# Attention and a squared-ReLU layer on one core: k and q of the first batch turned together, and a remainder made by a product with a negative identity

## The chip, the cores and the metric

The program runs on one core of one Trainium2 chip. The metric is the time of one execution on the device in microseconds (us), the median of three runs. One more execution was taken with a profiler; all rows shown are from it.

## What is computed

```python
rms = sqrt(mean(x * x, axis=-1, keepdims=True) + 1e-06)       # for q and k, over 64 elements
q_n, k_n = q / rms * g_q, k / rms * g_k
scores = q_n @ k_n.T / 8
attn = softmax(scores)                                        # over the keys
x = (attn @ v), heads side by side                            # 3584 x 768
h = maximum(x @ w_in, 0)                                      # 3584 x 2048
out = (s * h * h + b) @ w_out                                 # 3584 x 768
```

There are 8 batches of 12 heads, each with 448 rows of 64 elements. All is float32, `w_in` and `w_out` come as float64 and are read as pairs of 32-bit words.

## The kernel before

**Pairs and slots.** Two heads make a pair, six pairs a batch, 48 pairs in all; `j` is the head of a pair, 0 (the even head) or 1. The order of all work is written out by hand in slots: a pair has eight (`W = 8`), slot 8p the first of pair p, four for each head, and 22 slots lead in. In slot s TensorE is given, in this order: the two `st` products of slot s (`score_t`, L451 and L454: scores with the keys on the partitions), the transposes of a turn if one is due (L278), the `sh` product of slot s + 10 (`score`, L410: scores with the queries on the partitions, for their maximum), and `av` of slot s - 2 (`weigh`, L513: the exponents times v). ScalarE is given first the exponent of slot s (L466), which waits for `st` of the same slot. Then come the next steps of the jobs already begun, then the jobs that begin in this slot, then on VectorE `maximum` of slot s + 10 (L421), and last the jobs called late, the conversions of w_in among them. Every engine runs its queue in the order given.

**Products of two parts.** TensorE takes float32 in a faster rounded form (float32r). So k and q are split in a high part, the rounded copy, and a low part, the difference: `ka` holds k_hi in its partitions 0 to 63 and k_lo in 64 to 127, `qa` q_hi in both halves, and `qb` q_lo.

**The first batch and three pairs more (pairs 0 to 8)** read q and k by rows: `load_rows`, then `norm_rows` squares on ScalarE (L261), sums on VectorE (L266), makes the inverse root and multiplies on GpSimd (L269 to L271). `turn`, fourteen slots ahead of the head's first slot, transposes them on TensorE into two banks of PSUM, `tk` of k and `tk` of q, by four transposes of 112 x 64 each. `split_turned` follows in three steps, one a slot: ScalarE copies k_hi (L286) and scales q_hi (L287); ScalarE scales q_hi again into the other half (L289) and VectorE subtracts k_lo (L290); VectorE makes q_lo (L293). Then the banks are free. PSUM has eight banks, handed out from one list in the order in which they come free; `st`, `sh`, `av`, `tk`, `ph` and the words of w_in (`bits`) share it.

**Beside it** w_in is converted in 24 pieces: four steps on VectorE (L135, L138, L140, L143) and two on ScalarE (L136, L149) over five slots; `PACE` is the list of slots in which a piece begins. From slot 56 on a slot also carries six `ffn_in` products (L208) of the batch before. Pairs from 9 on (`NR`) are read in another way (`load`, `norm`, L348, L353). `split_x` (L562, L563) splits a group of the attention's result for `ffn_in`; `invert` and `divide` come before it and divide by the softmax sums.

Of the kernel before, what the change touches and what calls it, by code (L numbers as in the profile page):

```python
# [39 lines left out]
OUT = (92, *range(110, 141, 6), *(48 * b + i for b in range(3, 8) for i in range(14, 43, 7)))  # L40


@with_exitstack
def attention_then_relu2_ffn(
# [197 lines left out]
    if True:  # L242
# [8 lines left out]

        def load_rows(p, j):
            tag = f"{('kq', 'rb')[p % 2]}{j}"
            raw = raws[p, j] = ap.tile([QC, 2, NQ, D], F32, tag=tag, name=f"rows{p}_{j}")
            nc.sync.dma_start(raw, rows0[p, :, j])

        def norm_rows(p, j):
            raw = raws[p, j].rearrange("p t c d -> p (t c) d")
            n = 2 * NQ
            sq = lp.tile([QC, n, D], F32, tag="al", bufs=2, name=f"sq{p}_{j}")  # L260
            S.activation(  # L261
                sq.rearrange("p i d -> p (i d)"), raw.rearrange("p i d -> p (i d)"), AF.Square
            )
            yield
            ssq = ap.tile([QC, n], F32, tag="ssq", bufs=2, name=f"ssq{p}_{j}")
            V.tensor_reduce(out=ssq, in_=sq, op=ALU.add, axis=AX.X)  # L266
            yield
            ri = ap.tile([QC, n], F32, tag="ri", bufs=2, name=f"ri{p}_{j}")
            G.tensor_scalar(ri, ssq, 1.0 / D, 1e-6, ALU.mult, ALU.add)  # L269
            G.tensor_tensor(ri, ri, mhalf[:QC, :n], ALU.pow)  # L270
            G.tensor_tensor(raw, raw, ri.unsqueeze(2).broadcast_to([QC, n, D]), ALU.mult)  # L271

        def turn(p, j):
            raw = raws.pop((p, j))
            for t in range(2):
                tk, bank = psum(f"tk{p}_{j}_{t}")
                for c in range(NQ):
                    T.transpose(  # L278
                        tk[:D, c * QC : (c + 1) * QC], raw[:, t, c], ident[:QC, :QC]
                    )  # L280
                tks[p, j, t] = tk[:D, :SEQ], bank

        def split_turned(p, j):
            n, a = p % 2, slice(j * SEQ, (j + 1) * SEQ)
            (k, k_bank), (q, q_bank) = (tks.pop((p, j, t)) for t in range(2))
            S.copy(ka[n][:D, a], k)  # L286
            S.activation(qa[n][:D, a], q, AF.Copy, scale=gqk[:D])  # L287
            yield
            S.activation(qa[n][D:, a], q, AF.Copy, scale=gqk[:D])  # L289
            V.tensor_tensor(ka[n][D:, a], k, ka[n][:D, a].bitcast(F32), ALU.subtract)  # L290
            free.append(k_bank)
            yield
            V.scalar_tensor_tensor(  # L293
                qb[n][:D, a], q, gqk[:D], qa[n][:D, a].bitcast(F32), ALU.mult, ALU.subtract
            )
            free.append(q_bank)

        def load_kq(p, j):
            t = kqs[p, j] = ap.tile([P, 2, SEQ], F32, tag=f"kq{j}", name=f"kq{p}_{j}")
# [324 lines left out]
                next(g)  # L624
                loaded.append(g)

        def convert(n):


            g = loaded[0] if n == 0 else turning[0]  # L630
            if n == 0:
                turning.append(loaded.pop(0))
            for _ in range((2, 1, 1, 2, 1)[n]):
                next(g, None)
            if n == 4:
                turning.pop(0)

        turning = []

        late = (convert, convert_out, invert)  # L640

        fill = iter(())

# [11 lines left out]
        for p in range(NPAIR):  # L655
            s0 = W * p
            if p >= NR:
                at(s0 - 32, load, p)
                at(s0 - 28, norm, p)
                at(s0 - 24, keep, p)  # L660
            for j in range(2):
                s1 = s0 + 4 * j
                if p >= NR:
                    at(s1 - 19, load_kq, p, j)
                    at(s1 - 19, spread, p, j)
                    at(s1 - 15, scale, p, j)
# [15 lines left out]
            at(s0 + 13, invert, p)  # L682
            at(s0 + 14, divide, p, 1)
            at(s0 + 16, divide, p, 2)
            at(s0 + 18, divide, p, 3)
        for b in range(B):
            for g in range(NP):
                at(end(b + 1) - (2 if b < B - 1 else 4) + g, split_x, b, g)
        for s_ in (FIRST, FIRST + 3):
            at(s_, load_piece)  # L690
        for s_ in PACE:
            for n in range(5):
                at(s_ + n, convert, n)
            at(s_ + 3, load_piece)

        for s_ in OUT:
            at(s_ - 5, load_out)
# [371 lines left out]
```

## Time and profile before

| what | value |
| --- | --- |
| median of three runs | 1401.3 us (1400.87 to 1402.17) |
| the profiled execution | 1402.48 us |
| its span, from first to last instruction | 1400.7 us |
| TensorE (PE) busy | 1379.6 us, 98% |
| VectorE (DVE) busy | 1038.5 us, 74% |
| ScalarE (ACT) busy | 868.8 us, 62% |
| GpSimd (POOL) busy | 1021.7 us, 73% |
| mean granted TensorE clock | 0.996 |

PE is the matmul, PEld the load of its weights (they overlap), SP the engine that issues the DMAs. A row of the timeline has the start in us from the span's start, the duration, engine, source line, operation, the tiles written and read, shapes and count, and in brackets the idle time before it and what ended it. A row of a view by line has the count, the busy time and the mean of one in ns, and then the idle time before them with its releasers. The lines (L451) are those of the kernel before; in the kernel after, the same statements stand 3 to 19 lines lower.

### The profile page before, as it was taken

How to read it: one execution, taken by the hardware profiler on the slowest of the kernel's cores; microseconds unless marked ns; L12 is line 12 of the kernel's file. 1: busy time of each engine (PE TensorE's matmuls, PEld its weight loads, DVE VectorE, ACT ScalarE, POOL GpSimd, SP SyncE). 2: the span in 40 equal slices, each digit the busy share in tenths (PEclk: the TensorE clock that was granted, in tenths of full speed). 3: DMA queues.
4: the chain of work that ended last, by engine and by line, in shares of the span. 5: the costliest groups of instructions: out<-in, count | busy, mean ns of one | idle time of the engine just before them, and what ended most of it. 6: DMA issues, size and time to landing. Idle time of an engine off the chain costs nothing. (4 is left out here: it accounts for less than half of the span.)

```text
span 1400.7 us, 22180 instructions
## 1 busy us (share of the span) xinstructions
PE 1379.6 (98%) x6976; PEld 1262.0 (90%) x6976; DVE 1038.5 (74%) x1603; ACT 868.8 (62%) x1658; POOL 1021.7 (73%) x940
## 2 busy tenths in 40 slices
PE   7999999999999999999999999999999999999998
PEld 5666888999999899999989989989999999999998
DVE  8999786888888778788788778565766665666655
ACT  5776666777777776776777777654544444444443
POOL 7687788777877787777787776267767777577763
PEclk8999999999999999999999999999999999999999
DMA  5566886777677677677677766354434333233331
GB/s 148 133 174 175 258 242 192 220 239 226 190 238 217 200 235 218 189 228 239 198 219 214 225 188 204 94 160 150 118 91 121 99 99 98 84 120 98 98 97 62
DMA packets 209253, 237.95 MB, mean 170 GB/s; under 512 B 72848, under 2 KB 187024, under 8 KB 209136
## 3 DMA queue, kind: packets, MB, share of 16 engines
q1 hardware_dynamic: 209136, 236.54, 57.6%
q8 instruction: 55, 0.90, 0.3%
q14 instruction: 62, 0.51, 0.1%
HBM read 178.00 MB, written 47.11 MB: 161 GB/s over the span
## 5 line engine op out<-in xcount | busy, mean ns | idle before, releaser
L208 PE MATMUL ph<-x,wih 128*128 128x448 f32 x1536 | 491.7, 366 | 0.5 <-DVE x L563 0.5
L848 PE MATMUL m<-t,gh 128*128 128x384 f32 x1568 | 399.3, 335 | 0.2
L208 PEld LDWEIGHTS ph<-x,wih 128*128 128x128 f32 x1536 | 288.6, 188 | 30.8 <-issue 6.7
L421 DVE TENSOR_REDUCE nmx<-sh 112x1 fp32r<-112x448 f32 x384 | 236.6, 618 | 85.3 <-PE sh L410 82.5
L208 PE MATMUL ph<-x,wil 128*128 128x448 f32 x768 | 294.0, 383 | 0.0
L848 PEld LDWEIGHTS m<-t,gh 128*128 128x128 f32 x1568 | 283.4, 188 | 1.0 <-DVE ot L863 0.9
L470 ACT ACTIVATE st<-st 128x448 f32<-128x448 f32 (+1 forms) x294 | 154.2, 524 | 192.9 <-PE st L454 189.9
L848 PE MATMUL m<-t,gl 128*128 128x384 f32 x784 | 262.6, 335 | 0.3 <-DVE gl L830 0.3
L829 ACT CAST gh<-g 128x896 fp32r<-128x896 f32 x112 | 105.4, 942 | 178.2 <-POOL g L819 178.2
L830 DVE TENSOR_TENSOR gl<-g,gh 128x896 fp32r<-128x896 f32 x112 | 127.7, 1141 | 107.2 <-ACT gh L829 107.2
L815 POOL TENSOR_TENSOR g<-g 128x256 f32<-128x256 f32 x112 | 94.6, 845 | 113.5 <-DVE g L814 113.5
L513 PE MATMUL av<-ah,vs 128*128 128x448 f32 x576 | 164.9, 367 | 0.8 <-DVE al L491 0.5
L451 PE MATMUL st<-qa,ka 128*128 128x448 f32 (+1 forms) x384 | 159.1, 414 | 4.1 <-DVE nmx L421 4.0
L208 PEld LDWEIGHTS ph<-x,wil 128*128 128x128 f32 x768 | 144.3, 188 | 17.9 <-issue 6.7
L478 ACT CAST ah<-st 128x448 fp32r<-128x448 f32 (+1 forms) x294 | 156.8, 533 | 1.3
L555 POOL TENSOR_TENSOR u<-uz,zb 64x448 f32<-64x448 f32 x96 | 126.7, 1320 | 42.1 <-DMA zb<-z_d 38.3
L410 PE MATMUL sh<-ka,qa 128*112 128x448 f32 x384 | 145.5, 382 | 3.6 <-DVE ka L290 1.8
L848 PEld LDWEIGHTS m<-t,gl 128*128 128x128 f32 x784 | 147.1, 188 | 0.6 <-DVE gl L830 0.6
L491 DVE TENSOR_TENSOR al<-st,ah 128x448 fp32r<-128x448 f32 x216 | 132.7, 614 | 18.7 <-ACT ah L478 15.8
L454 PE MATMUL st<-qb,kb 128*128 128x448 f32 (+1 forms) x384 | 140.4, 366 | 0.0
L394 POOL TENSOR_TENSOR ka<-kq,ka 64x448 fp32r<-64x448 f32 x78 | 95.5, 1224 | 57.0 <-ACT ka L391 52.3
L819 POOL TENSOR_TENSOR g<-g 128x256 f32<-128x256 f32 x112 | 125.9, 1124 | 0.0
(93 smaller groups left out, 2398.2 us busy)
## 6 DMA issues: line engine op xcount, KB each, us to landing
kq<-in_dram SPq DMA_DIRECT2D x78, 448.0 KB, 4.9
rb<-i_d SPq DMA_DIRECT2D x78, 448.0 KB, 5.9
r_d<-r SPq DMA_DIRECT2D x128, 224.0 KB, 3.1
raw<-in_dram SPq DMA_DIRECT2D x39, 448.0 KB, 5.1
raw<-r_d SPq DMA_DIRECT2D x64, 256.0 KB, 2.8
w64i<-in_dram SPq DMA_DIRECT2D x24, 512.0 KB, 4.7
w64o<-in_dram SPq DMA_DIRECT2D x32, 384.0 KB, 4.6
kb<-ka SPq DMA_DIRECT2D x96, 112.0 KB, 3.3
```

Of the source, the lines that this page charges most:

```text
L208: T.matmul(ph[:, :SEQ], w[:, cc, f0 : f0 + P], xs[b, cc][:, part, :], start=n == 0, stop=n == 3 * NCC - 1,)
L410: T.matmul(sh[:QC, :SEQ], qa[p % 2][:, a].rearrange("k (p c) -> k c p", c=NQ)[:, c], ka[p % 2][:, a], start=True, stop=True,)
L421: V.tensor_reduce(out=nmxs[p][:, c : c + 1], in_=sh[:QC, :SEQ], op=ALU.max, axis=AX.X, negate=True)
L451: T.matmul(st[:rows, :SEQ], ka[n][:, keys], qa[n][:, q], start=True, stop=False)
L454: T.matmul(st[:rows, :SEQ], kb[n][:, keys], qb[n][:, q], start=False, stop=True,)
L470: S.activation(st[:rows, :SEQ], st[:rows, :SEQ], AF.Exp)
L478: S.copy(ah[:rows], sts[i][0][:rows, :SEQ])
L491: V.tensor_tensor(al, st[:rows, :SEQ], ah[:rows].bitcast(F32), ALU.subtract)
L513: T.matmul(av[:, :SEQ], x, a, start=kc == 0 and m == 0, stop=kc == 3 and m == len(todo) - 1,)
L555: G.tensor_tensor(u[a], uzs.pop((p, j))[a], zb[a], ALU.mult)
L830: V.tensor_tensor(gl, g9[:, 1:8], gh.bitcast(F32), ALU.subtract)
L848: T.matmul(to, g[:, sa], w, start=m == 0 and n == 0, stop=m == NM - 1 and n == 2,)
```

## The change

**The joint turn.** `rows0` is laid out so that k and q of one row lie side by side, and `turn` transposes 112 x 128 at a time: four transposes and one bank, with k in its partitions 0 to 63 and q in 64 to 127. The bank is given back when all of `split_turned` has read it.

**k_lo in PSUM.** For the even head of pairs 2 to 8 (`in_bank`), `less_hi` adds the product of `ka` and a negative identity (`less`, 64 x 64 in a 128 x 128 tile of zeros) to the turned bank, so that k - k_hi stands where k stood; ScalarE then copies it to `ka` (L311 of the kernel after), in the third step of `split_turned` in place of the subtraction in the second. The product is called late in the slot of the second step, that is, behind `sh` and ahead of `av`, and writes all 128 partitions of the bank (adding zeros to q).

**The order.** `norm_rows` comes two slots earlier from pair 2 on; the first `load` of `NR` ten slots earlier; three of the later pieces of w_in begin later and all of them keep their order; the first piece of w_out eight slots later; `invert` and `divide` of the first five pairs one to three slots later; the last `split_x` of batch 0 one slot later.

```diff
-PACE = (-15, -10, *range(1, 61, 5), *range(59, 89, 3))
+PACE = (-15, -10, *range(1, 56, 5), 60, 63, 66, 69, 72, 74, 77, 79, 82, 84, 87)
...
+    less = cpool.tile([P, P], F32R, name="less")
+    G.memset(less.bitcast(F32), 0.0)
+    S.activation(less[: P // 2, : P // 2], ident[: P // 2, : P // 2], AF.Copy, scale=-1.0)
...
         def turn(p, j):
             raw = raws.pop((p, j))
-            for t in range(2):
-                tk, bank = psum(f"tk{p}_{j}_{t}")
-                for c in range(NQ):
-                    T.transpose(
-                        tk[:D, c * QC : (c + 1) * QC], raw[:, t, c], ident[:QC, :QC]
-                    )
-                tks[p, j, t] = tk[:D, :SEQ], bank
+            tk, bank = psum(f"tk{p}_{j}")
+            for c in range(NQ):
+                T.matmul(
+                    tk[:, c * QC : (c + 1) * QC],
+                    raw[:, c].rearrange("p t d -> p (t d)"),
+                    ident[:QC, :QC],
+                    start=c == 0, stop=not in_bank(p, j) and c == NQ - 1, is_transpose=True,
+                    skip_group_check=True,
+                )
+            tks[p, j] = tk, bank
+
+        def in_bank(p, j):
+            return p >= 2 and j == 0
+
+        def less_hi(p, j):
+            n, a = p % 2, slice(j * SEQ, (j + 1) * SEQ)
+            T.matmul(
+                tks[p, j][0][:, :SEQ], less, ka[n][:, a],
+                start=False, stop=True, skip_group_check=True,
+            )
...
             S.copy(ka[n][:D, a], k)
-            S.activation(qa[n][:D, a], q, AF.Copy, scale=gqk[:D])
+            S.activation(qa[n][D:, a], q, AF.Copy, scale=gqk[D:])
             yield
-            S.activation(qa[n][D:, a], q, AF.Copy, scale=gqk[:D])
-            V.tensor_tensor(ka[n][D:, a], k, ka[n][:D, a].bitcast(F32), ALU.subtract)
-            free.append(k_bank)
+            S.activation(qa[n][:D, a], q, AF.Copy, scale=gqk[D:])
+            if not in_bank(p, j):
+                V.tensor_tensor(ka[n][D:, a], k, ka[n][:D, a].bitcast(F32), ALU.subtract)
             yield
+            if in_bank(p, j):
+                S.copy(ka[n][D:, a], k)
...
-                at(s0 - 32, load, p)
+                at(s0 - (42 if p == NR else 32), load, p)
...
-                    at(s1 - 21, norm_rows, p, j)
+                    at(s1 - (21 if p < 2 else 23), norm_rows, p, j)
                     at(s1 - 14, turn, p, j)
                     at(s1 - 13, split_turned, p, j)
+                    if in_bank(p, j):
+                        at(s1 - 12, less_hi, p, j)
```

How it moves instructions, at the even head of pair 5. On TensorE, from the `st` products of slot 26 to those of slot 28 and what follows, before:

```order
L278 MATMUL tk5_0_0_958<-ident_66,rows5_0_670 64x112 x4
L278 MATMUL tk5_0_1_963<-ident_66,rows5_0_670 64x112 x4
L410 MATMUL sh36_968<-ka0_198,qa0_200 112x448
L513 MATMUL av3_0_975<-e24_913,vf3_814 128x448
L451 MATMUL st27_977<-qa1_201,ka1_199 128x448
L454 MATMUL st27_977<-qb1_205,kb1_203 128x448
L410 MATMUL sh37_992<-ka0_198,qa0_200 112x448
L513 MATMUL av3_0_975<-e25_934,vf3_814 128x448
L451 MATMUL st28_997<-qa1_201,ka1_199 128x448
L454 MATMUL st28_997<-qb1_205,kb1_203 128x448
L410 MATMUL sh38_1008<-ka0_198,qa0_200 112x448
```

and after:

```order
L280 MATMUL tk5_0_915<-ident_66,rows5_0_642 128x112 x4
L429 MATMUL sh36_920<-ka0_201,qa0_203 112x448
L532 MATMUL av3_0_927<-e24_874,vf3_779 128x448
L470 MATMUL st27_929<-qa1_204,ka1_202 128x448
L473 MATMUL st27_929<-qb1_208,kb1_206 128x448
L429 MATMUL sh37_946<-ka0_201,qa0_203 112x448
L532 MATMUL av3_0_927<-e25_891,vf3_779 128x448
L470 MATMUL st28_951<-qa1_204,ka1_202 128x448
L473 MATMUL st28_951<-qb1_208,kb1_206 128x448
L429 MATMUL sh38_959<-ka0_201,qa0_203 112x448
L294 MATMUL tk5_0_915<-ka1_202,less_74 128x448
L532 MATMUL av3_0_927<-e26_904,vf3_779 128x448
```

Eight transposes became four, and the product (L294) stands behind `sh38` and ahead of `av` of slot 26. In the built program it waits for ScalarE's second q copy of this head (L306 below).

On ScalarE, from the exponent of slot 27 (`e27`) to that of slot 29, before:

```order
L466 ACTIVATE e27_980<-st27_977 128x448
L286 CAST ka1_199<-tk5_0_0_958 64x448
L287 ACTIVATE qa1_201<-tk5_0_1_963,gqk_214 64x448
L261 ACTIVATE sq6_0_990<-rows6_0_839 112x512
L466 ACTIVATE e28_1000<-st28_997 128x448
L289 ACTIVATE qa1_201<-tk5_0_1_963,gqk_214 64x448
L466 ACTIVATE e29_1017<-st29_1014 128x448
L149 CAST wih1_716<-wai7_1011 128x512
```

and after:

```order
L485 ACTIVATE e27_932<-st27_929 128x448
L303 CAST ka1_202<-tk5_0_915 64x448
L304 ACTIVATE qa1_204<-tk5_0_915,gqk_217 64x448
L485 ACTIVATE e28_954<-st28_951 128x448
L306 ACTIVATE qa1_204<-tk5_0_915,gqk_217 64x448
L485 ACTIVATE e29_969<-st29_966 128x448
L311 CAST ka1_202<-tk5_0_915 64x448
L264 ACTIVATE sq6_1_976<-rows6_1_879 112x512
L152 CAST wih1_682<-wai7_963 128x512
```

The squares of `norm_rows` left the place ahead of `e28`, and the copy of k_lo (L311) came in behind `e29`.

On VectorE, around the same head, before:

```order
L290 TENSOR_TENSOR ka1_199<-tk5_0_0_958,ka1_199 64x448
L266 TENSOR_REDUCE ssq6_0_1004<-sq6_0_990 112x8
L421 TENSOR_REDUCE nmx4_889<-sh38_1008 112x1
L143 SCALAR_TENSOR_TENSOR wai7_1011<-wih1_716,bits7_971 128x512
L293 SCALAR_TENSOR_TENSOR qb1_205<-tk5_0_1_963,gqk_214,qa1_201 64x448
L421 TENSOR_REDUCE nmx4_889<-sh39_1026 112x1
```

and after:

```order
L440 TENSOR_REDUCE nmx4_846<-sh38_959 112x1
L146 SCALAR_TENSOR_TENSOR wai7_963<-wih1_682,bits7_923 128x512
L312 SCALAR_TENSOR_TENSOR qb1_208<-tk5_0_915,gqk_217,qa1_204 64x448
L440 TENSOR_REDUCE nmx4_846<-sh39_980 112x1
L269 TENSOR_REDUCE ssq6_1_990<-sq6_1_976 112x8
```

The subtraction (L290) is gone, and q_lo (L312), which waited for the second q copy (L289), waits in the built program for the copy of k_lo (L311). At an odd head VectorE's subtraction (L308) stays; it now waits for the second q copy (L306), where L290 waited for L286.

More of the change, by code (lines that the diff above doesn't have):

```diff
@@ L32 @@
 FILL = (2, 2, 2)
-PACE = (-15, -10, *range(1, 61, 5), *range(59, 89, 3))
+PACE = (-15, -10, *range(1, 56, 5), 60, 63, 66, 69, 72, 74, 77, 79, 82, 84, 87)
 GAP = 2
 STEPS = {0: 2, 1: 3, 2: 4, 3: 5, 5: 6, 6: 7, 8: 8, 9: 9, 11: 10, 12: 11, 13: 12}
-OUT = (92, *range(110, 141, 6), *(48 * b + i for b in range(3, 8) for i in range(14, 43, 7)))
+OUT = (100, *range(110, 141, 6), *(48 * b + i for b in range(3, 8) for i in range(14, 43, 7)))
 @with_exitstack
@@ L253, in load_rows @@
             tag = f"{('kq', 'rb')[p % 2]}{j}"
-            raw = raws[p, j] = ap.tile([QC, 2, NQ, D], F32, tag=tag, name=f"rows{p}_{j}")
+            raw = raws[p, j] = ap.tile([QC, NQ, 2, D], F32, tag=tag, name=f"rows{p}_{j}")
             nc.sync.dma_start(raw, rows0[p, :, j])
         def norm_rows(p, j):
-            raw = raws[p, j].rearrange("p t c d -> p (t c) d")
+            raw = raws[p, j].rearrange("p c t d -> p (c t) d")
             n = 2 * NQ
@@ L274, in turn @@
             raw = raws.pop((p, j))
-            for t in range(2):
-                tk, bank = psum(f"tk{p}_{j}_{t}")
-                for c in range(NQ):
-                    T.transpose(
-                        tk[:D, c * QC : (c + 1) * QC], raw[:, t, c], ident[:QC, :QC]
-                    )
-                tks[p, j, t] = tk[:D, :SEQ], bank
+            tk, bank = psum(f"tk{p}_{j}")
[16 more added lines that the diff above has]
+            )
         def split_turned(p, j):
             n, a = p % 2, slice(j * SEQ, (j + 1) * SEQ)
-            (k, k_bank), (q, q_bank) = (tks.pop((p, j, t)) for t in range(2))
+            tk, bank = tks[p, j]
+            k, q = tk[:D, :SEQ], tk[D:, :SEQ]
             S.copy(ka[n][:D, a], k)
-            S.activation(qa[n][:D, a], q, AF.Copy, scale=gqk[:D])
+            S.activation(qa[n][D:, a], q, AF.Copy, scale=gqk[D:])
             yield
-            S.activation(qa[n][D:, a], q, AF.Copy, scale=gqk[:D])
-            V.tensor_tensor(ka[n][D:, a], k, ka[n][:D, a].bitcast(F32), ALU.subtract)
-            free.append(k_bank)
+            S.activation(qa[n][:D, a], q, AF.Copy, scale=gqk[D:])
+            if not in_bank(p, j):
+                V.tensor_tensor(ka[n][D:, a], k, ka[n][:D, a].bitcast(F32), ALU.subtract)
             yield
+            if in_bank(p, j):
+                S.copy(ka[n][D:, a], k)
             V.scalar_tensor_tensor(
-                qb[n][:D, a], q, gqk[:D], qa[n][:D, a].bitcast(F32), ALU.mult, ALU.subtract
+                qb[n][:D, a], q, gqk[D:], qa[n][D:, a].bitcast(F32), ALU.mult, ALU.subtract
             )
-            free.append(q_bank)
+            free.append(bank)
         def load_kq(p, j):
@@ L625, in load_piece, with convert @@
                 loaded.append(g)
-        def convert(n):
-            g = loaded[0] if n == 0 else turning[0]
+        def convert(n, at_):
             if n == 0:
-                turning.append(loaded.pop(0))
+                turning[at_] = loaded.pop(0)
             for _ in range((2, 1, 1, 2, 1)[n]):
[L634 to L640, printed above, removed]
+                next(turning[at_], None)
+        turning = {}
+        late = (convert, convert_out, invert, less_hi)
         fill = iter(())
@@ L681, in attention_then_relu2_ffn @@
                 at(s0 + 3, split_v_rest, p)
[L682 to L685, printed above, removed]
+            wait = (0, 0, 0, 0) if p >= NP else (0, 1, 1, 1) if p == NP - 1 else (1, 2, 2, 3)
+            at(s0 + 13 + wait[0], invert, p)
+            for n in range(3):
+                at(s0 + 14 + 2 * n + wait[n + 1], divide, p, n + 1)
         for b in range(B):
             for g in range(NP):
-                at(end(b + 1) - (2 if b < B - 1 else 4) + g, split_x, b, g)
+                at(end(b + 1) - (2 if b < B - 1 else 4) + g + (b == 0 and g == NP - 1), split_x, b, g)
         for s_ in (FIRST, FIRST + 3):
@@ L692, in attention_then_relu2_ffn @@
             for n in range(5):
-                at(s_ + n, convert, n)
-            at(s_ + 3, load_piece)
+                at(s_ + n, convert, n, s_)
+            at(s_ + (3 if s_ < 60 else 2), load_piece)
         for s_ in OUT:
@@ L1052 @@
     rows0 = _np.stack([a.reshape(n, 2, 4, s // 4, d)[:9] for a in (k, q)], 2)
-    rows0 = rows0.transpose(0, 4, 1, 2, 3, 5)
+    rows0 = rows0.transpose(0, 4, 1, 3, 2, 5)
     laid = [kq, rows, rows0, vs, g] + [_np.asarray(inputs[x]) for x in _INS]
```

## The prediction

> **What bounds the kernel now.** I read the stretches of the windows view first, then who waited for whom on TensorE, then the timeline of single slots. After its first batch the kernel is a full TensorE: the busy time in stretches of 20 us, with the columns PE, PEld, DVE, ACT, POOL (each with its instructions), clock, DMA share and GB/s:
>
> ```profile
> core 0: us, PE busy (x) PEld busy (x) DVE busy (x) ACT busy (x) POOL busy (x), PEclk, DMA share, GB/s
> ...
> 20.00:40.00 20.00, 18.16 (x75) 12.98 (x74) 19.68 (x34) 15.87 (x31) 13.76 (x17) 0.87 0.48 129
> 40.00:60.00 20.00, 18.62 (x82) 12.99 (x80) 18.33 (x32) 14.47 (x30) 14.21 (x17) 1.00 0.46 120
> ...
> 100.00:120.00 20.00, 17.35 (x74) 11.36 (x72) 17.80 (x32) 14.86 (x29) 15.81 (x19) 1.00 0.67 165
> 120.00:140.00 20.00, 17.94 (x74) 13.76 (x73) 17.83 (x27) 12.35 (x24) 13.33 (x13) 1.00 0.71 188
> 140.00:160.00 20.00, 20.00 (x87) 16.21 (x87) 14.33 (x25) 12.31 (x24) 16.25 (x15) 1.00 0.89 269
> ```
>
> From 140 us on TensorE has no idle time. The change adds and removes nothing there, so the end moves by what the first batch gains or loses. In the first batch VectorE is as full as TensorE. The start of a slot is the weight load of its first `st` product (L451); the first row here is slot 3, the second slot 60, and 61 and 62 follow:
>
> ```profile
> 28.97 0.19 PEld L451 LDWEIGHTS st<-qa,ka 128*128 128x128 f32 x1 [0.19 <-PE sh L410]
> ...
> 134.07 0.19 PEld L451 LDWEIGHTS st<-qa,ka 128*128 128x128 f32 x1
> ...
> 136.66 0.19 PEld L451 LDWEIGHTS st<-qa,ka 128*128 128x128 f32 x1
> 139.22 0.19 PEld L451 LDWEIGHTS st<-qa,ka 128*128 128x128 f32 x1
> ```
>
> Slot 3 to slot 60 is 105.1 us. How long TensorE needs for it by itself comes from three rows: a slot without a turn, slot 28, and a turn of eight transposes, slot 30:
>
> ```profile
> 71.19 0.19 PEld L451 LDWEIGHTS st<-qa,ka 128*128 128x128 f32 x1 [0.19 <-issue]
> 71.56 0.19 PEld L454 LDWEIGHTS st<-qb,kb 128*128 128x128 f32 x1 [0.19 <-issue]
> 71.77 0.28 PEld L410 LDWEIGHTS sh<-ka,qa 128*112 128x112 f32 x1
> 71.97 0.39 PEld L513 LDWEIGHTS av<-e,vf 128*128 128x128 f32 x2
> 72.54 0.19 PEld L451 LDWEIGHTS st<-qa,ka 128*128 128x128 f32 x1 [0.19 <-ACT qa L287]
> 73.91 0.19 PEld L451 LDWEIGHTS st<-qa,ka 128*128 128x128 f32 x1 [0.19 <-issue]
> 74.49 0.89 PEld L278 LDWEIGHTS tk<-ident,rows 112*64 112x64 f32 x8
> ```
>
> A slot is 1.36 us ((73.91 - 71.19) / 2), a turn adds 0.89, and a slot with six `ffn` products is 2.57 ((139.22 - 134.07) / 2). The 57 slots are 53 of the first kind (3 to 55), with 13 turns (slots 6, 10 ... 54), and four of the last (56 to 59): 72.1 + 11.6 + 10.3 = 94.0 us. So TensorE lost 11.1 us to waits, and mostly VectorE ended them, as TensorE's own list of waits for these 105 us says (engine, line, releaser: us, times, longest):
>
> ```profile
> PEld st L451 <- DVE nmx L421: 7.3, 10, 2.6
> ...
> PEld sh L410 <- DVE wai L143: 1.8, 2, 1.2
> ```
>
> A PSUM bank comes free when `maximum` or a conversion of w_in has read it, and VectorE is late with that. The two largest single ones, slots 47 and 59, and what stood ahead of the first:
>
> ```profile
> 102.31 0.95 ACT L348 ACTIVATE raw<-raw 128x896 f32<-128x896 f32 x1 [1.64 <-DMA raw<-in_dram]
> ...
> 105.03 0.19 PEld L451 LDWEIGHTS st<-qa,ka 128*128 128x128 f32 x1 [2.61 <-DVE nmx L421]
> ...
> 131.58 0.19 PEld L451 LDWEIGHTS st<-qa,ka 128*128 128x128 f32 x1 [2.23 <-DVE nmx L421]
> ```
>
> **The change part by part.** The profiled execution took 1402.48 us, a span of 1400.7 and 1.8 outside it; the median of the three runs is 1401.3, so I work out a difference and put it on the median.
>
> *The joint turn.* Eight transposes with 64 columns of weights become four with 128. What a step of TensorE's queue costs here is the weight load:
>
> ```profile
> L278 PEld LDWEIGHTS tk<-ident,rows 112*64 112x64 f32 x104 | 10.3, 111 | 2.0 <-DVE nmx L421 0.6
> ...
> L451 PEld LDWEIGHTS st<-qa,ka 128*128 128x128 f32 x58 | 11.0, 189 | 15.8 <-DVE nmx L421 7.3 <-issue 4.3 <-ACT qa L287 1.7
> ...
> L278 PE MATMUL tk<-ident,rows 112*64 112x112 f32 x104 | 12.3, 259 | 0.4 <-DVE nmx L421 0.4
> ```
>
> 8 x 0.111 = 0.89 becomes 4 x 0.189 = 0.76: 0.13 a turn, **-1.7** over 13 turns. The bounds: a joint load at the price of a small one (0.111) gives 13 x 0.444 = -5.8; four transposes at the recorded 0.259 of one give 1.04 a turn, +1.9. I take 0.189, since it is a load of the same 128 columns. The Trainium skill (TensorE: Matmul & The Clock Gate, "LDWEIGHTS (loading the stationary operand)") prices a load by its columns alone, columns / 1.2 ns. By that eight loads of 64 cost what four of 128 cost, and this term would be 0 instead of -1.7; the trace disagrees, 111 ns for 64 columns being far over half of 189 for 128. The five turns ahead of slot 3 are counted at nothing: they wait for `norm_rows` on GpSimd. So are the memset and the negative identity, in the wait for the first rows.
>
> *The product with the negative identity*, seven times (pairs 2 to 8, slots 4, 12 ... 52). Its own time is a product of 448 columns, 0.20 (71.97 - 71.77). It stands in TensorE's queue between `sh` and `av` of its slot, and it may not write the bank before ScalarE has read q from it for the second time. That copy stands behind the `exponent` of the same slot, which waits for the `st` product issued 0.6 us earlier. In slot 28, TensorE's second `st` product, and then ScalarE from slot 27's exponent on:
>
> ```profile
> 71.76 0.36 PE L454 MATMUL st<-qb,kb 128*128 128x448 f32 x1
> ```
>
> ```profile
> 70.87 0.54 ACT L466 ACTIVATE e<-st 128x448 f32<-128x448 f32 x1 [0.84 <-PE st L454]
> 71.31 0.51 ACT L286 CAST ka<-tk 64x448 fp32r<-64x448 f32 x1
> 71.72 0.63 ACT L287 ACTIVATE qa<-tk,gqk 64x448 fp32r<-64x448 f32 x1
> 72.25 0.62 ACT L261 ACTIVATE sq<-rows 112x512 f32<-112x512 f32 x1
> 72.77 0.53 ACT L466 ACTIVATE e<-st 128x448 f32<-128x448 f32 x1
> 73.32 0.63 ACT L289 ACTIVATE qa<-tk,gqk 64x448 fp32r<-64x448 f32 x1
> ```
>
> `norm_rows` (L261) moves two slots earlier, so its row goes from this place and the exponent runs when both ScalarE (72.25) and `st` (72.12) are done: 72.25. The second q copy starts 0.55 later (73.32 - 72.77) and takes 0.63: 73.43. The product could have started at 71.97. So TensorE waits 1.4 us, plus 0.2 of its own, plus about 0.1 for a weight load that no product covers after a wait (an estimate: half of 0.19): 1.7 x 7 = **+11.9**. Behind it in TensorE's queue stand `av` of slot 26 and all of slot 29; ScalarE then waits for `st` of slot 29, and VectorE for `sh`. Bounds: no wait at all, 7 x 0.2 = +1.4; above, the next term.
>
> *Conversions of w_in on ScalarE* fall into the slot ahead of the product in slots 11, 19 and 51, between the first copies and the exponent. Such a step is 0.62 to 0.67:
>
> ```profile
> L136 ACT ACTIVATE wih<-w64i 128x512 fp32r<-128x512 f32 x11 | 7.4, 674 | 0.0
> ...
> L149 ACT CAST wih<-wai 128x512 fp32r<-128x512 f32 x11 | 6.8, 617 | 8.9 <-DVE wai L143 8.8
> ```
>
> The copies there leave ScalarE no slack against a slot of 1.36 (70.87 to 72.25, 1.38, from one exponent to the next without L261), so each adds about 0.6: **+1.8**, between 0 and 2.0.
>
> *The waits that go.* VectorE loses seven subtractions (0.618 each, 4.3 us), and up to slot 60 the conversion that began in slot 56 with half of that of slot 59 (six steps of 0.69, 4.1 us):
>
> ```profile
> L290 DVE TENSOR_TENSOR ka<-tk,ka 64x448 fp32r<-64x448 f32 x14 | 8.7, 618 | 1.0 <-ACT ka L286 0.6
> ...
> L135 DVE TENSOR_SCALAR bits<-w64i 128x512 int32<-128x512 int32 x12 | 8.2, 680 | 0.0
> ```
>
> The rows of pair 9 are asked for ten slots earlier, which takes away the 1.64 of DMA in front of slot 47's wait. While TensorE stands at the product, VectorE catches up. Against that stands a new wait: the q_lo step of an even head (L312) now follows k_lo's copy on ScalarE (L311), and `maximum` of its slot, a sum of squares and a conversion queue behind it on VectorE; TensorE needs the banks that these free two slots later. That copy ends about one exponent and one copy after `st` of slot 29, some 1 us, and VectorE, having caught up, stands for 1 to 2 us. An odd head's subtraction likewise follows the second q copy. Of the 11.1 us I keep 2.3 and let 8.8 go: **-8.9**, rounded. Bounds: 0.5 kept (one short wait in all), or 6 kept (over half of what VectorE and the banks cost now).
>
> *At nothing.* ScalarE's seven copies (0.51 each) come in time that it waits anyway behind the product. The conversions that now come later are wanted at slot 92 (the last starts at 87, five slots of 2.57 ahead). The divisions, one to three slots later, meet their split in slot 60 and the first product with it in slot 61; if that cover is gone TensorE waits about a us there. SP's queue carries the same transfers, pair 9's first load ten slots earlier.
>
> The sum: -1.7 + 11.9 + 1.8 - 8.9 = **+3.1 us**: 1405.6 for the profiled execution and 1404.4 on the median, 0.22% slower. A difference under 0.2% (2.8 us) can hardly be told from none here.
>
> **The rivals.** *The waits just change places*: the same chain, but nearly all 11.1 us go, since VectorE always has time to catch up. With 0.5 kept the sum is +1.3 and the time 1402.6. For it: VectorE's work falls by 8.4 us while TensorE's stretch grows. Against: the two new waits of VectorE on ScalarE.
>
> *VectorE becomes the bound through the wait for L311.* It is idle up to 1.6 us in each of seven pairs, 11 us, where it was free for 6.4 of the 80 us of the four first-batch rows above; if it comes to L312 more than a slot late, `maximum` falls behind and the bank waits stay, 6 kept: +6.8, 1408.1. It decides from the point where VectorE's rest after a product is shorter than its wait at L312.
>
> *The product does not wait* (the faster side): its operands are there when TensorE comes to it, because TensorE comes late for other reasons. Then 7 x 1.4 = 9.8 fall away: -6.7, 1394.6. For it: TensorE did lose 11.1 us. Against: none of that was in slots of this kind; slot 28 above ran its bare 1.36, and the exponent cannot run ahead of its own `st`. It decides if the second q copy ends within 0.1 us of `sh`. The cheap bound of the joint turn (-5.8) would bring a part of this by itself, to about 1400.3.
>
> That the change doesn't do what it says I leave out: the built program has the seven products, the seven copies and half the transposes.
>
> **How the numbers follow.** The forecast, with 1.5 to 5 us lost, gets 0.50, of which 0.16 lies under 2.8. The waits that change places get 0.22, all within 0.2%; VectorE as the bound 0.13, slower; the faster side 0.15. So faster 0.15, no change 0.38, slower 0.47. The forecast's own range is 1402.8 to 1406.3. The range, 1399.2 to 1408.5, takes in the slower rival and the cheap joint turn, and leaves out the faster rival's core and a tail above.
>
> **What would show it.** Right: `PEld tk` with the product's line waits for ScalarE's L306 seven times by about 1.4 us; the load of a joint turn is 0.19; the 1.64 of DMA and the 2.6 and 2.2 are gone; slot 60 starts about 3 us later than 134.07, and every later slot as before. Wrong: products that wait under half a us; waits for `nmx` still over 5 us (then VectorE is the bound); joint loads at 0.11; or a difference that arises after slot 60.

## The result, and the profile after

The changed kernel took 1420.57 us (median of 4 runs, 1418.04 to 1422.94) beside 1401.53 us for the kernel before on the same chip: a ratio of 1.0139, 95% interval 1.0124 to 1.0154 (the quotient of the two medians is 1.0136, inside it). It is slower, by 19 us where 3 were forecast, and outside the range. The profiled execution took 1421.25 us with a span of 1419.1.

The starts of slots 3, 60 and 108 in the changed kernel (weight load of the slot's first `st` product, now L470):

```profile
29.17 0.19 PEld L470 LDWEIGHTS st<-qa,ka 128*128 128x128 f32 x1 [0.19 <-ACT e L485]
...
147.70 0.19 PEld L470 LDWEIGHTS st<-qa,ka 128*128 128x128 f32 x1
...
272.03 0.19 PEld L470 LDWEIGHTS st<-qa,ka 128*128 128x128 f32 x1
```

Slots 3 to 60 take 118.5 us instead of 105.1 (+13.4). The same rows of the kernel before give 120.4 us for slots 60 to 108 (its slot 108 starts at 254.44), and now 124.3 (+4.0). What lies before slot 3 (+0.2) and after slot 108 (+0.8) is nearly unchanged. So there are two losses, a large one where it was looked for and a smaller one where nothing was expected.

The windows view, columns as in the prediction (TensorE is the first busy figure, the granted clock stands behind the fifth): two rows of the kernel before, and then the changed kernel.

```profile
60.00:80.00 20.00, 20.00 (x89) 14.54 (x88) 19.03 (x35) 17.02 (x35) 15.16 (x17) 1.00 0.63 169
80.00:100.00 20.00, 19.41 (x86) 13.77 (x85) 18.59 (x33) 15.74 (x32) 15.36 (x17) 1.00 0.58 157
```

```profile
40.00:60.00 20.00, 17.66 (x64) 11.79 (x62) 14.62 (x27) 15.26 (x29) 9.92 (x12) 0.91 0.41 113
60.00:80.00 20.00, 16.71 (x57) 10.54 (x55) 14.50 (x26) 13.22 (x26) 11.11 (x13) 0.91 0.46 117
80.00:100.00 20.00, 15.88 (x60) 10.55 (x59) 15.70 (x28) 14.64 (x28) 13.92 (x16) 1.00 0.60 163
...
120.00:140.00 20.00, 17.41 (x64) 12.07 (x62) 14.71 (x24) 14.04 (x26) 13.92 (x13) 0.91 0.60 165
```

No engine is full any more. VectorE, at 17.8 to 19.0 us of 20 in these stretches before, is at 14.5 to 15.7; it lost work (the seven subtractions), but it also stands still. And the granted clock, 1.00 in these stretches before, is 0.91 in three of them. The lists of waits between slots 3 and 60 say who stood for whom, TensorE's first, then VectorE's (releaser: us in total, times, longest):

```profile
PE tk L294 <- ACT qa L306: 13.0, 7, 2.4
...
PEld tk L294 <- ACT qa L306: 15.0, 7, 2.7
PEld sh L429 <- DVE nmx L440: 2.7, 5, 0.9
...
PEld st L470 <- DVE nmx L440: 1.0, 4, 0.3
```

```profile
DVE qb L312 <- ACT ka L311: 18.4, 7, 5.1
DVE ka L308 <- ACT qa L306: 4.1, 3, 1.7
```

In the kernel before, VectorE's list for the same slots has for the q_lo step (there L293) only this:

```profile
DVE qb L293 <- ACT qa L289: 0.6, 2, 0.3
```

The forecast's wait is there: the product (L294) seven times behind the second q copy (L306). But VectorE stands for 18.4 us at L312, up to 5.1 at a time, where 1 to 2 us each were supposed. The worst of the seven, slot 20:

```profile
64.23 0.62 ACT L152 CAST wih<-wai 128x512 fp32r<-128x512 f32 x1 [0.69 <-DVE wai L146]
64.87 0.54 ACT L485 ACTIVATE e<-st 128x448 f32<-128x448 f32 x1
...
65.44 0.63 ACT L306 ACTIVATE qa<-tk,gqk 64x448 fp32r<-64x448 f32 x1
...
66.12 0.74 PE L294 MATMUL tk<-ka,less 128*128 128x448 f32 x1 [2.43 <-ACT qa L306]
...
67.41 0.34 PEld L470 LDWEIGHTS st<-qa,ka 128*128 128x128 f32 x1 [0.41 <-issue]
...
69.20 0.54 ACT L485 ACTIVATE e<-st 128x448 f32<-128x448 f32 x1 [3.13 <-PE st L473]
...
69.77 0.53 ACT L311 CAST ka<-tk 64x448 fp32r<-64x448 f32 x1
...
70.33 0.69 DVE L312 SCALAR_TENSOR_TENSOR qb<-tk,gqk,qa 64x448 fp32r<-64x448 f32 x1 [5.12 <-ACT ka L311]
```

It is one ring of three engines. A conversion of w_in on ScalarE waits for VectorE, so the exponent is late, so the q copy, so the product; TensorE stands 2.43 us, then does the next `st` slowly (a load of 0.34 instead of 0.19, at a granted clock of 0.50); ScalarE stands 3.13 us for that `st`, k_lo's copy comes behind its exponent, and VectorE, at the end of the ring, stands 5.12 us for the copy. How much of this is the clock's is told below, with w_out's piece.

The second loss, at slots 106 and 107: VectorE, GpSimd and TensorE in the changed kernel.

```profile
262.91 3.06 POOL L574 TENSOR_TENSOR u<-uz,zb 64x448 f32<-64x448 f32 x2 [0.16 <-DMA zb<-z_d]
...
262.94 0.55 DVE L173 SCALAR_TENSOR_TENSOR wao<-w64o,wao 128x384 f32<-128x384 f32 x1
263.41 1.58 DVE L393 SCALAR_TENSOR_TENSOR kq<-kq,gqk,rb 128x448 f32<-128x448 f32 x1
264.91 1.55 DVE L582 TENSOR_TENSOR x<-u,x 128x448 fp32r<-128x448 f32 x1
...
267.14 0.99 PE L532 MATMUL av<-ah,vs 128*128 128x448 f32 x2 [2.21 <-DVE al L510]
```

L173 is a step of w_out's first piece, which the change moved from slot 92 to slot 100. Behind it VectorE's L393 and L582 run beside GpSimd's division, at 1.58 and 1.55 us, and TensorE then waits 2.21 us for the subtraction behind them. Whether the piece is the cause is tried below too.

### The profile page after: what moved, and what is told of

The parts are those of the page before. It is cut to its first block, busy times and chain, and to the rows that moved or that the text cites. A ratio compares the mean times of both kernels' runs of the same rounds, so it can differ in the third digit from the quotient of the medians.

```text
span 1419.1 us, 22040 instructions
## 1 busy us (share of the span) xinstructions
PE 1383.8 (98%) x6911; PEld 1261.4 (89%) x6911; DVE 1033.2 (73%) x1596; ACT 879.1 (62%) x1666; POOL 1023.1 (72%) x941
## 5 line engine op out<-in xcount | busy, mean ns | idle before, releaser
L470 PE MATMUL st<-qa,ka 128*128 128x448 f32 (+1 forms) x384 | 161.0, 419 | 0.8 <-DVE qb L312 0.8
```

What stands on the lines that cost most here:

```text
L470: T.matmul(st[:rows, :SEQ], ka[n][:, keys], qa[n][:, q], start=True, stop=False)
```

## The experiments

**Theory A** is the chain at the product: the seven products wait, and VectorE's L312 and the banks are late behind them. **Rival B**: the shared bank costs by itself, since its readers on ScalarE and VectorE are put one after the other, product or not. **Rival C**: the new order costs. **Rival D**: VectorE's wait for k_lo's copy, not the product's own wait. Starts are taken from the same rows as above, "3 to 60" and "60 to 108" are their differences; two profiled executions of the same program up to slot 60 (the changed kernel, and that with w_out's piece at slot 92) differ there by 2.7 us, so smaller differences of one stretch prove little alone.

| kernel | ratio to before, 95% interval | slots 3, 60, 108 start at | 3 to 60 | 60 to 108 |
|---|---|---|---|---|
| before | 1 | 28.97, 134.07, 254.44 | 105.1 | 120.4 |
| changed | 1.0139, 1.0124 to 1.0154 | 29.17, 147.70, 272.03 | 118.5 | 124.3 |
| no product | 1.0080, 1.0063 to 1.0097 | 29.92, 139.75, 262.52 | 109.8 | 122.8 |
| second q copy early | 1.0051, 1.0036 to 1.0066 | 29.70, 136.80, 261.50 | 107.1 | 124.7 |
| product ahead of second q copy | 1.0073, 1.0058 to 1.0088 | 29.31, 138.70, 263.11 | 109.4 | 124.4 |
| w_out's piece at slot 92 | 1.0105, 1.0089 to 1.0120 | 29.34, 145.21, 265.96 | 115.9 | 120.8 |
| before, joint turn alone | 1.0150, 1.0135 to 1.0165 | 29.81, 151.11, 272.11 | 121.3 | 121.0 |
| new order alone | 0.9989, 0.9980 to 0.9999 | 28.68, 128.20, 252.33 | 99.5 | 124.1 |
| readers apart | 1.0019, 1.0009 to 1.0028 | 29.14, 131.58, 254.84 | 102.4 | 123.3 |
| readers apart, no product | 1.0025, 1.0015 to 1.0034 | 28.99, 131.74, 254.30 | 102.8 | 122.6 |
| joint turn into two banks, no product | 1.0017, 1.0008 to 1.0026 | 28.91, 131.24, 256.15 | 102.3 | 124.9 |
| new order, w_out at 92 | 0.9962, 0.9950 to 0.9975 | 28.24, 127.38, 248.06 | 99.1 | 120.7 |
| readers apart, `sh` later, w_out at 92 | 0.9990, 0.9980 to 0.9999 | 28.76, 129.76, 250.28 | 101.0 | 120.5 |
| the same, no product | 0.9998, 0.9989 to 1.0007 | 28.06, 131.06, 251.60 | 103.0 | 120.5 |

### Without the product

```
         def in_bank(p, j):
-            return p >= 2 and j == 0
+            return False
```

> The changed kernel without the product: VectorE makes k_lo of every head again, the joint turn and the new order stay. Theory A (the chain around the product: the product waits about 2.2 us, seven times, for the second q copy of its own slot, and VectorE's L312 and the banks come late behind it): slots 3 to 60 take about 101 to 106 us instead of 118.5, no `PEld tk` wait for ScalarE, the half-clock stretches between 40 and 132 us go, and the 4 us lost at slots 106 and 107 stay: 1406 to 1411 us. Rival B (one bank for k and q, and its readers on two engines one after the other, cost the time with or without a product): TensorE's waits for banks stay, 114 us or more from slot 3 to 60, 1415 us or more. Rival C (the new order of norms, conversions and divisions costs the time): 1415 us or more too.

Measured: 1411.96 us, slots 3 to 60 in 109.8. It lies between the two: 8.7 us come back, but the stretch is still 4.7 us longer than before, though TensorE has less to do. The granted clock is 1.00 from 40 to 140 us, as A had it. VectorE's and TensorE's waits, and one of the first kind in time order:

```profile
DVE ka L308 <- ACT qa L306: 8.7, 7, 1.8
...
PE sh L429 <- DVE nmx L440: 9.8, 13, 1.2
```

```profile
63.46 0.63 ACT L306 ACTIVATE qa<-tk,gqk 64x448 fp32r<-64x448 f32 x1
...
64.13 0.62 DVE L308 TENSOR_TENSOR ka<-tk,ka 64x448 fp32r<-64x448 f32 x1 [1.44 <-ACT qa L306]
```

L308 reads the lower 64 partitions of the bank and k_hi, L306 the upper 64, and neither uses what the other makes; but they touch one bank, and the program lets L308 wait. Before, k had a bank of its own and L290 waited for ScalarE only 0.6 us in all. This speaks for A and B together.

### The second q copy early

```
             S.activation(qa[n][D:, a], q, AF.Copy, scale=gqk[D:])
-            yield
             S.activation(qa[n][:D, a], q, AF.Copy, scale=gqk[D:])
+            yield
```

> The changed kernel with the second q copy (L306) in the same step as the first copies, one exponent earlier on ScalarE: the product stays, but what it waits for was done one slot before. Theory A: the product starts without a wait, TensorE keeps only its 0.2 us, seven times, and L308 of odd heads does not wait either; the copies delay that slot's exponent chain by at most 0.6 us; what VectorE loses at L312 behind L311 stays. Slots 3 to 60 in 103 to 109 us, 1407 to 1413 us in all. Rivals B and C: the wait only moves to the banks, 114 us or more, 1415 us or more.

Measured: 1408.63 us, 107.1 for slots 3 to 60, in the range of A: 11.4 us come back with all the work in place. "Without a wait" was wrong, since three copies and an exponent take ScalarE longer than a slot (0.51, 0.63, 0.63 and 0.54 us in the kernel before, against 1.36):

```profile
PE tk L294 <- ACT qa L305: 6.0, 7, 1.6
```

```profile
DVE qb L312 <- ACT ka L311: 10.1, 7, 2.2
```

### The product ahead of the second q copy

```
             yield
+            if in_bank(p, j):
+                less_hi(p, j)
             S.activation(qa[n][:D, a], q, AF.Copy, scale=gqk[D:])
...
-                    if in_bank(p, j):
-                        at(s1 - 12, less_hi, p, j)
```

> The changed kernel with the product ahead of the second q copy: in TensorE's queue it stands right behind the slot's two `st` products, and the q copy, behind the exponent anyway, reads the bank after it. Nothing else is changed; k_lo is still copied one slot later and VectorE's L312 still follows that copy. Theory A: no wait at the product, slots 3 to 60 in 103 to 109 us, 1407 to 1413 us. If instead the wait of VectorE's L312 for L311 is what costs (rival D), the banks stay late though the product is punctual: 112 us or more and 1414 us or more. Rivals B and C: 1415 us or more.

Measured: 1411.78 us, 109.4. Products that wait 3.1 us in all instead of 13.0 give back 9.1 us, as A has it, though the stretch lies just above A's range (103 to 109). 8.0 us of VectorE's wait behind k_lo's copy (here L313) remain. That leaves room for D, whose share this run doesn't separate:

```profile
PE tk L294 <- ACT qa L304: 3.1, 6, 1.2
```

```profile
DVE qb L314 <- ACT ka L313: 8.0, 7, 2.1
```

### w_out's first piece back at slot 92

```
-OUT = (100, *range(110, 141, 6), *(48 * b + i for b in range(3, 8) for i in range(14, 43, 7)))
+OUT = (92, *range(110, 141, 6), *(48 * b + i for b in range(3, 8) for i in range(14, 43, 7)))
```

> The changed kernel with the first piece of w_out converted from slot 92 on, as before the change, instead of from slot 100. If the 4 us lost at slots 106 and 107 come from that piece running beside the splits of x of batch 1 on VectorE and ScalarE: slots 60 to 108 take 120.4 instead of 124.3 us, the half-clock stretch at 265 us is gone, and the time is about 1416.6 us, with slots 3 to 60 unchanged. If they come from the divisions moved later: no difference, 1420.5 us.

Measured: 1416.20 us, and 120.8 us for slots 60 to 108 instead of 124.3. The divisions are where the change put them, so the second loss is the piece's. With it at slot 92 the same step L393 takes 0.68 us, although GpSimd's division runs beside it here too; the first half of that division then takes 2.45 us, where it took 1.59 in the changed kernel (the profile's spans of GpSimd are rough):

```profile
260.51 2.45 POOL L574 TENSOR_TENSOR u<-uz,zb 64x448 f32<-64x448 f32 x1
```

```profile
260.75 0.68 DVE L393 SCALAR_TENSOR_TENSOR kq<-kq,gqk,rb 128x448 f32<-128x448 f32 x1
```

So the piece costs the time, and behind it VectorE's steps are slow; why VectorE is the slow one there, and GpSimd here, is not shown.

All kernels of the table with the piece at 92 take 120.4 to 121.0 there, all with it at 100 take 122.6 to 124.9. Of these, the three with clock 1.00 from 240 to 280 us (no product, and readers apart with and without it) take 122.6 to 123.3, and the five with a slow stretch there 124.1 to 124.9. So the piece costs 2.2 to 2.9 us at clock 1.00, and the slow clock behind the wait adds the rest.

That the slots 3 to 60 would be unchanged was missed: they took 115.9 us, not 118.5, in the same program with the same waits of the product (12.9 us, seven, up to 2.4). What differs is the clock, 1.00 from 40 to 140 us in this execution. The row of 60 to 80 us, and the ring at slot 20:

```profile
60.00:80.00 20.00, 15.97 (x58) 10.12 (x58) 15.85 (x29) 14.99 (x28) 13.31 (x15) 1.00 0.50 130
```

```profile
65.20 0.47 PE L294 MATMUL tk<-ka,less 128*128 128x448 f32 x1 [2.44 <-ACT qa L306]
...
66.92 0.54 ACT L485 ACTIVATE e<-st 128x448 f32<-128x448 f32 x1 [1.77 <-PE st L473]
...
68.05 0.69 DVE L312 SCALAR_TENSOR_TENSOR qb<-tk,gqk,qa 64x448 fp32r<-64x448 f32 x1 [3.77 <-ACT ka L311]
```

TensorE's wait is the same, and VectorE's is still the longest of the three; with the slow clock ScalarE's and VectorE's were 1.4 us longer.

### The kernel before with the joint turn alone

Against the kernel before:

```
-            for t in range(2):
-                tk, bank = psum(f"tk{p}_{j}_{t}")
...
+            tk, bank = psum(f"tk{p}_{j}")
+            for c in range(NQ):
+                T.matmul(
+                    tk[:, c * QC : (c + 1) * QC],
+                    raw[:, c].rearrange("p t d -> p (t d)"),
+                    ident[:QC, :QC],
+                    start=c == 0, stop=c == NQ - 1, is_transpose=True,
```

> The kernel before with the joint turn alone: one bank for k and q of a head, VectorE subtracts for every head, and norms, conversions, divisions and w_out stand where they stood before; no product. Theory B (in the shared bank the subtraction of k follows the second q copy on ScalarE, while before it followed the k copy alone): VectorE waits for that copy about 1.2 to 1.5 us in half the heads and more, slots 3 to 60 take 108 to 111 us (105.1 before, 109.8 without the product in the new order), 1404 to 1407 us. Theory C (the new order costs, not the bank): the joint turn's 5 us are a gain, slots 3 to 60 in 100 to 102 us, 1396 to 1398 us.

Measured: 1421.68 us, 121.3 for slots 3 to 60. C falls: the joint turn in the old order is not a gain of 5 us but a loss of 16, without any product and far above what B expected (108 to 111 us). The granted clock, 0.91 in three of the stretches between 40 and 140 us, has a part in it. The two lists of waits, VectorE's and TensorE's:

```profile
DVE ka L294 <- ACT qa L293: 14.5, 9, 3.1
```

```profile
PE sh L413 <- DVE nmx L424: 13.0, 10, 2.0
```

L294 is the subtraction here and L293 the second q copy: the wait of the run without the product, and larger. Why the old order makes it larger was not tried.

### The new order alone

Against the changed kernel, with the lines of before in `turn`, `split_turned`, the layout of the rows and the table of jobs; some of them:

```
-            tk, bank = psum(f"tk{p}_{j}")
...
+            for t in range(2):
+                tk, bank = psum(f"tk{p}_{j}_{t}")
...
-late = (convert, convert_out, invert, less_hi)
+late = (convert, convert_out, invert)
```

> The changed kernel's order (norms two slots earlier, conversions after slot 56 later, divisions later, w_out's first piece from slot 100) with the turn and the split of before: eight transposes, two banks, VectorE subtracts, no product. Theory B: slots 3 to 60 take 103 to 106 us as before, and slots 60 to 108 the 4 us more that w_out's piece costs: 1403 to 1406 us. Theory C: slots 3 to 60 take 110 us or more, 1408 us or more.

Measured: 1399.49 us, below what either theory expected. Slots 3 to 60 take 99.5 us: the order gains 5.6 us, and loses 3.8 of them again after slot 60. (The description of the change has three later pieces of w_in begin later; the list `PACE` moves the last eleven, by one to four slots.) TensorE's wait for the banks, 7.3 us before, is halved:

```profile
PEld st L451 <- DVE nmx L421: 3.7, 8, 1.0
```

### The joint turn into two banks

Against the run without the product:

```
+            for t in range(2):
+                tk, bank = psum(f"tk{p}_{j}_{t}")
+                for c in range(NQ):
+                    T.matmul(
+                        tk[:, c * QC : (c + 1) * QC],
+                        raw[:, c].rearrange("p t d -> p (t d)"),
...
+            k, q = k[:D, :SEQ], q[D:, :SEQ]
```

> The version without the product (VectorE subtracts, steps where the change has them) with the joint turn made twice, into two banks: k is read from one, q from the other, so the subtraction follows the k copy alone. TensorE does eight loads of 128 columns a turn instead of four, 0.55 us more. Theory B (the order of the readers of the one bank is the loss, not the joint turn itself): slots 3 to 60 in 100 to 104 us although TensorE has 7 us more to do than with one bank (109.8 there); 1402 to 1407 us. If the shape of the turn costs by itself, 112 us or more.

Measured: 1403.68 us, 102.3 for slots 3 to 60, where the one bank took 109.8, and VectorE's waits behind ScalarE's copies are gone:

```profile
DVE qb L308 <- ACT qa L301: 0.3, 1, 0.3
```

This kernel has the joint shape, the new order and twice the transposes, and differs from the run without the product only in the second bank and the transposes that fill it. So the shared bank is what costs, and B is shown. The next two runs show that it costs by the order of its readers.

### The readers apart, with and without the product

```
             yield
-            S.activation(qa[n][:D, a], q, AF.Copy, scale=gqk[D:])
             if not in_bank(p, j):
-                V.tensor_tensor(ka[n][D:, a], k, ka[n][:D, a].bitcast(F32), ALU.subtract)
+                S.activation(qa[n][:D, a], q, AF.Copy, scale=gqk[D:])
             yield
             if in_bank(p, j):
+                S.activation(qa[n][:D, a], q, AF.Copy, scale=gqk[D:])
                 S.copy(ka[n][D:, a], k)
+            else:
+                V.tensor_tensor(ka[n][D:, a], k, ka[n][:D, a].bitcast(F32), ALU.subtract)
+            yield
             V.scalar_tensor_tensor(
```

> The changed kernel with the readers of the shared bank put apart: for an even head the second q copy and k_lo's copy come one slot after the product, for an odd head VectorE's subtraction comes one slot after the second q copy, and q_lo of both one slot later still. The product then waits only for copies of the slot before, VectorE only for copies of the slot before. Theory A with B (order of the bank's readers is the whole loss): the product waits 0 to 0.8 us, VectorE's waits behind ScalarE fall under 4 us in all, slots 3 to 60 in 98 to 104 us; with the 4 us after slot 60, 1400 to 1406 us. Rival D (a bank held one slot longer makes the banks short, or ScalarE with its 14 us more work is itself late): TensorE waits for banks instead, 106 us or more, 1408 us or more.

> The changed kernel without the product (VectorE subtracts for all heads, as in the first run) and with the subtraction one slot after the second q copy, q_lo one slot after that. Theory B: VectorE no longer waits behind ScalarE (8.7 us without this), slots 3 to 60 fall from 109.8 to 100 to 104 us, and with the 2 to 4 us after slot 60 the time is 1401 to 1406 us. Rival C or D: 108 us or more, 1409 us or more.

Measured: 1403.68 and 1404.38 us, 102.4 and 102.8 for slots 3 to 60, both in the theory's range. With the product, the ratio falls from 1.0139 to 1.0019, 17 of the 19 us, with all work and the one bank kept; the waits of the first list are nearly gone, and a smaller one is new, `sh` behind k_lo's copy of the slot just before:

```profile
PE tk L294 <- ACT qa L304: 1.0, 5, 0.2
...
PEld sh L432 <- ACT ka L311: 4.8, 7, 1.5
```

```profile
DVE qb L315 <- ACT ka L311: 2.3, 5, 1.3
```

The pair also prices the product when nothing waits for it: the two differ by 0.7 us in time and 0.3 in the stretch, nothing that can be told.

### A version that beats both

This is the new order alone with the first piece at slot 92.

```
-OUT = (100, *range(110, 141, 6), *(48 * b + i for b in range(3, 8) for i in range(14, 43, 7)))
+OUT = (92, *range(110, 141, 6), *(48 * b + i for b in range(3, 8) for i in range(14, 43, 7)))
```

> The new order alone as before, with the turn, split and banks of the kernel before, and w_out's first piece back at slot 92. Theory: the order's gain of 5.6 us up to slot 60 (99.5 us) stays and the 3.8 us lost after it with that piece at slot 100 go: slots 60 to 108 in 120.4 us, 1395 to 1397 us, ratio to before about 0.996. If the late loss belongs to the later divisions, 1399.5 us.

Measured: 1395.74 us, ratio 0.9962 (0.9950 to 0.9975), 99.1 and 120.7 us: as expected, and the fastest of all. It has neither the joint turn nor the product.

### `sh` one slot later

Against the readers apart with and without the product, both with w_out's first piece at slot 92:

```
-AHEAD = 10
+AHEAD = 9
...
-                at(s1 - 6, shift, p, j)
+                at(s1 - 5, shift, p, j)
```

> The version with the readers of the bank put apart (product kept), with `sh` and its `maximum` nine slots ahead instead of ten, the shift one slot later, and w_out's first piece at slot 92. `sh` then no longer follows k_lo's copy or subtraction of the slot just before (6.9 us of TensorE's load waits there). Theory: slots 3 to 60 fall from 102.4 to 96 to 100 us, slots 60 to 108 take 120.4: 1392 to 1397 us. Rival: with `sh` one slot later the shift's transfer is late for `st`, or the waits go to `maximum`'s banks: 102 us or more, 1399 us or more.

> The same without the product: VectorE subtracts for all heads one slot after the second q copy, `sh` nine slots ahead, w_out's first piece at slot 92. It prices the product once nothing waits for it: VectorE has seven subtractions more (4.3 us), TensorE seven products less (1.4 us). Theory: slots 3 to 60 in 97 to 101 us, within 2 us of the version with the product; 1393 to 1398 us. If VectorE is the bound there, 2 to 4 us more than with the product.

Measured: 1399.53 and 1400.47 us, 101.0 and 103.0 for slots 3 to 60, both slower than expected and slower than the version with eight transposes. The waits of `sh` for k_lo only made room for others; without the product for `maximum`'s banks, that is, VectorE:

```profile
PEld st L473 <- DVE nmx L443: 12.8, 24, 1.3
```

So in none of the versions tried do the 5 us that the joint turn saves TensorE shorten the time: in this stretch TensorE waits for VectorE and ScalarE instead. Why the version with the product stays 1.9 us behind the eight transposes there (its list spreads over `nmx` 3.7, `e` 3.0 and the product 2.8) was not settled.

## Why the prediction was wrong, point by point

Between slots 3 and 60 it forecast +3.1 us and got +13.4; of this the new order brings -5.6, the joint bank +10.3 on top of it (99.5 to 109.8), the product in its place +8.7 (109.8 to 118.5; 6.1 by the execution at clock 1.00). The shares hold for this sequence: in the old order the joint bank alone cost 16.2 (105.1 to 121.3).

- **The joint turn** (-1.7 forecast). A slot with a bare turn in the changed kernel, and one in the kernel with two joint turns:

```profile
84.25 0.19 PEld L470 LDWEIGHTS st<-qa,ka 128*128 128x128 f32 x1 [0.19 <-issue]
...
84.83 0.54 PEld L280 LDWEIGHTS tk<-ident,rows 112*128 112x128 f32 x4
...
86.10 0.19 PEld L470 LDWEIGHTS st<-qa,ka 128*128 128x128 f32 x1 [0.19 <-issue]
```

```profile
60.59 0.19 PEld L466 LDWEIGHTS st<-qa,ka 128*128 128x128 f32 x1 [0.19 <-ACT e L481]
...
61.17 0.92 PEld L282 LDWEIGHTS tk<-ident,rows 112*128 112x128 f32 x8
...
62.83 0.19 PEld L466 LDWEIGHTS st<-qa,ka 128*128 128x128 f32 x1 [0.19 <-issue]
```

The first slot takes 1.85 us, so a turn adds 0.49 instead of 0.89: TensorE has 13 x 0.40 = 5.2 us less to do, close to the cheap bound of 5.8. The 0.189 of `st` was the wrong row to borrow: eight transposes with 128 columns make the second slot 2.24 us, 0.88 more than a bare one, so one costs 0.11, as one with 64 columns did (0.89 / 8). But none of it was a gain in time.
- **The product** (+11.9 and +1.8 forecast). The seven slots take 26.6 us; less 7 x 1.36 that is +17.0. Three of them (4, 28, 44) are 1.8 longer than a bare slot, against 1.7 forecast: the mechanism and its size were right. The other four (12, 20, 36, 52) are 2.9 longer. Conversions were counted ahead of three of them, at the length of the conversion alone, and none ahead of slot 36; here one was itself late for VectorE, in slot 20 by 0.69 us and, ahead of slot 36, by 2.02:

```profile
94.77 0.62 ACT L152 CAST wih<-wai 128x512 fp32r<-128x512 f32 x1 [2.02 <-DVE wai L146]
...
97.49 0.63 ACT L306 ACTIVATE qa<-tk,gqk 64x448 fp32r<-64x448 f32 x1
```

- **The waits that go** (-8.9 forecast: "Of the 11.1 us I keep 2.3 and let 8.8 go"). This step failed (it was also entered as 8.9, though 11.1 - 2.3 is 8.8). TensorE's bare work is now 94.0 - 5.2 = 88.8 us; with the 17.0 of the products, 12.7 of the 118.5 are left as waits elsewhere, 10.4 more than kept. With 3.5 more saved by the turn and 3.3 more lost at the products that is the whole miss (10.4 + 3.3 - 3.5 = 10.2 of 10.3). In the execution at clock 1.00 the same sum leaves 10.8 instead of 12.7 (115.9 - 88.8 - 16.3), so by this one pair the slow clock has some 2 us of it (an estimate), and the rest stands. Two sentences failed in it. "VectorE, having caught up, stands for 1 to 2 us": it stood 18.4 / 7 = 2.6 us on average and up to 5.1, since its wait is the end of the chain through TensorE and ScalarE and not a short one beside it. And "An odd head's subtraction likewise follows the second q copy" was named and given no price, though it took 4.1 us of VectorE, the engine that was full, and needs no product: with every head's subtraction behind that copy the runs without the product lost 8.7 and 14.5 us of VectorE to it. The part on the order was sound: 5.6 us gained, 5.5 of waits left with the order alone (99.5 - 94.0).
- **The rival** of VectorE as the bound through L312 had the place right: VectorE loses most time at L312. Its sign did not come as written: TensorE's loads waited 3.7 us for `nmx` (2.7 and 1.0), not over 5. "6 kept" was too little by half against 12.7; the lists name only a part of these 12.7, so how they divide stays open.
- **After slot 60.** "The change adds and removes nothing there" failed too: the diff moves w_out's first piece by eight slots, a number in a table, and 3.5 to 3.6 of the +4.0 us go with it. No step priced it.
- **The clock** was not thought of. In steps of 0.5 us the granted clock of the changed kernel stands at 0.50 three times between slots 3 and 60, for 3.4 us each, from 48.8, 65.9 and 130.7 us on: in or soon behind the products' waits of 2.12, 2.43 and 2.11 us. The waits alone don't decide it: slot 36's of 2.23 us was not followed by a slow stretch, and the same program in the run with w_out's piece at slot 92 had the same waits at clock 1.00 and took 2.7 us less. The Trainium skill (TensorE: Matmul & The Clock Gate, "What's actually happening") says that the clock falls to half after at least one idle window of about 3.4 us. Here it falls though TensorE was never idle that long, so a window need not be wholly idle; the 3.4 us of the slow stretches fit its length. When it falls and when it doesn't was not settled.

## What to carry to other kernels

Merging two results into one PSUM bank merges their readers: ask of every engine that reads one half whether it now waits for the reader of the other half, and put those steps a slot apart before counting what TensorE saves. In a software pipeline with little slack, a new wait is not priced by its own length; follow it once round the ring, through the instruction queued behind it on each engine, back to where it began. And price every number that a table moves, the one far from the change too.

## What the runs showed of the hardware

- A transpose of 112 rows takes TensorE's queue as long with 128 columns of weights as with 64: eight of them lengthened a slot by 0.88 us and by 0.89. The weight load of an `st` product of 128 columns takes 0.19.
- VectorE and GpSimd slowed each other: VectorE's steps with two inputs in SBUF took 1.58 (L393) and 1.55 us (L582) beside GpSimd's division, and 0.68 and 0.61 at moments when GpSimd stood idle (in the run with w_out's piece at slot 92, and in the changed kernel); and where L393 took 0.68 beside a division, half of that division took 2.45 us, against 1.59 beside the slow L393. The Trainium skill (GPSIMD Engine Reference, "1. Specifications") says that GpSimd's SBUF interfaces are shared with VectorE, with contention for instructions with two SBUF inputs; the trace agrees.
- The waits between the halves of the bank are put there by the program; these runs don't show that the hardware needs them. The Trainium skill (PSUM — Partial Sum Buffer, "PSUM bank collisions raise a hardware error") says that two engines must be kept apart in the same bank and the same 32 partitions, and may use different quadrants of a bank at once; k and q lie in different ones. By that rule the 8.7 us of L308 behind L306 would not be needed. No run here shows it: letting those two go at once was not tried.
